# Weight forms and gated loads in SyncE's queue, the last gated stores in GpSimd's, at the turn between the two products of a gated layer

## The chip, the core and the metric

The kernel runs on one core of a Trainium2 chip. Its time is the device time of one launch in microseconds (us), as the median of several runs; the profile is of one further execution.

## What is computed

Attention with a positional decay, then two feed-forward layers on the 2304 tokens. The change lies in the last layer, whose reference is, word for word:

```
def _moe2_ref(x, w_in, w_out) -> np.ndarray:
    h = x @ w_in
    relu6 = np.clip(h + 3.0, 0.0, 6.0)
    g = h * relu6 / 6.0
    return (g @ w_out).astype(np.float32)
```

Here x is 2304 x 512, w_in 512 x 2048, w_out 2048 x 512. The weights of this layer come as 64-bit numbers and are decoded on the chip to 32-bit ones.

## The kernel before

**Two phases of one layer.** Both products of the layer are done in blocks of two by two with seven block products instead of eight (sums and differences of the blocks are formed first). Each 32-bit operand is split in a rounded high part and a low rest ("forms"); a block product is the sum of three TensorE products of these parts.

- In the first phase `unit(bi, k)` computes, for one of three groups of 768 tokens (bi) and one of eight slices of the hidden width (k), seven products of 6 matmuls each (line 1272, tiles `ws` and `xb`). Their results are collected by ACT and DVE (lines 1285 and 1291) and gated four times, `gate`: a relu on ACT (line 1298), a multiplication on DVE (line 1301), both in a tile `g` of a ring of six (`G_BUFS = 6`), and a store of 192 KB from that tile to the DRAM tensor `g_d` (line 1304). A tile of the ring is written again only when its store has landed. The last six units are those of the last two slices, k = 6 and 7, for bi = 0, 1 and 2; they have 24 gated stores.
- In the second phase `group(bi, t)` takes 128 columns of four gated blocks back from `g_d` (four loads `r11`, `r12`, `r21`, `r22`, line 1404; 512 KB each, in pieces of 512 bytes), forms sums (`n` and others, line 1412, on DVE), splits them (line 1424 on ACT, line 1428 on DVE or GpSimd) and multiplies them with the seven weight forms W0 to W6 (line 1447), 24 matmuls a product. There are nine groups. The results (`ob`) lie in tiles of the same ring `g` and are stored by line 1473.

**The weight forms** were made earlier and lie in DRAM: for W0, W1, W3 and W6 the unsplit blocks in `wt_d`, for W2, W4 and W5 (`SPLIT`) the split forms in `wp_d`. `weights(j)` loads each in three pieces. A piece of the first kind (256 or 384 KB, line 1353) goes to one of four staging places and is split by ACT and DVE (lines 1357 and 1360). A piece of the second kind (512 or 768 KB, line 1364) goes straight to its place. The places are the rooms of the first phase's operand forms `xb`, so a piece can come only when the last matmul that reads that room is done.

**Who issues, and in which order.** All instructions are collected with `plan.add(engine, us, function, ...)`, where `us` is a cost and `lag` the time until a result may be used; `emit` plays the plan through and writes each engine's instructions in the order of the planned starts. On the chip each engine's instructions then run in that order, each behind its waits. Before the change SyncE (SP) issues the gated stores, the gated loads and the output stores; GpSimd (POOL) issues all loads of weight forms. SyncE's transfers go through a hardware queue (q1 in the trace), GpSimd's through a software queue (q0); both run on the same 16 DMA engines.

Of the kernel before, what the change touches and what calls it, by code (L numbers as in the profile page):

```python
# [10 lines left out]
F32 = mybir.dt.float32  # L11
# [161 lines left out]
def dve(n):  # L173
    return 0.15 + 0.00104 * n
# [6 lines left out]
def act(n, extra=0.17):  # L181
    return extra + 0.00085 * n
# [6 lines left out]
def pe(n):  # L189
    return max(0.107, 0.000447 * n)  # L190
# [3 lines left out]
def kernel(ctx, tc, q, k, v, s, w_in, w_out, g_ln, w2_in, w2_out, out):  # L194
    nc = tc.nc
# [4 lines left out]
    P = 128  # L200
# [57 lines left out]
    def bank(key):  # L258
        return banks[plan.bank[key]]
# [124 lines left out]
    NK = KFF2 // 2  # L384
    T = {}
    wt_d = dram.tile([7, P, NK, 2 * P], F32, name="wt_d")
    wp_d = dram.tile([7, P, NK, 2, 2 * P], F32, name="wp_d")
    EARLY = (0,), (1, 2), (3, 4, 5)
    WT_PART = (0, 1, 2, 3, 4, 4, 6)
# [103 lines left out]
    plan = Plan()  # L493
# [619 lines left out]
    for b, share in enumerate(SHARES):  # L1113
        main = []
        if b == 0:
            first, second = pairs(False), pairs(True)
# [10 lines left out]
        while cost < share or in_sum:  # L1127
# [3 lines left out]
            c, f, _, in_sum = side.pop(pick)  # L1131
# [10 lines left out]
    g_d = dram.tile([NB, 2, 2, P, NK, W], F32, name="g_d")  # L1142
# [24 lines left out]
    def engine(name):  # L1167
        return {"DVE": nc.vector, "POOL": nc.gpsimd}[name]
# [15 lines left out]
    def x_form(bi, op):  # L1184
        return T[f"xb{bi}_{op}"]
# [74 lines left out]
    def unit(bi, k):  # L1260


        tag = f"{bi}_{k}"
        r = []

        def product(op, x, first):
            key = f"b{x}_{tag}"

            def mm():
                for kc in range(2):  # L1270
                    for i, (a, b) in enumerate(((0, 0), (1, 0), (0, 1))):
                        nc.tensor.matmul(bank(key)[:, :W], lhsT=T[f"ws{k}"][:, WS_OF[op], a, kc * P : (kc + 1) * P], rhs=x_form(bi, op)[:, b, kc, :],  # L1272
                                         start=(first and kc == 0 and i == 0), stop=(kc == 1 and i == 2), skip_group_check=not first)

            w = f"ws{k}"
            wk = {0: ["h0", "l0"], 1: ["h0", "l0"], 3: ["h768", "l768"], 5: ["s/h512", "s/l512"], 4: ["s/h512", "s/l512"]}.get(op, ["s/h0", "s/l0"])
            r.append(lambda: plan.add("PE", 6 * pe(W) + 0.01, mm, reads=[f"{w}/{y}" for y in wk] + [f"xb{bi}_{op}/{y}" for y in "hl"], writes=[key],
                                      bank=key if first else None))

        def keep(name, x):  # L1280
            key, to = f"b{x}_{tag}", f"{name}{tag}"

            def go():
                T[to] = pools["mid"].tile([P, W], F32, tag=name, name=to, bufs=2)
                nc.scalar.copy(T[to], bank(key)[:, :W])  # L1285

            r.append(lambda: plan.add("ACT", act(W), go, reads=[key, "second"], writes=[to], new=[(name, 2, to)]))

        def plus(name, x):
            key, to = f"b{x}_{tag}", f"{name}{tag}"  # L1290
            r.append(lambda: plan.add("DVE", dve(W), lambda: nc.vector.tensor_add(T[to], T[to], bank(key)[:, :W]), reads=[key, to], writes=[to]))

        def gate(o, h, src_key, src, eng="DVE"):
            g = f"g{tag}_{o}{h}"

            def relu():
                T[g] = pools["g"].tile([P, W], F32, tag="g", name=g, bufs=G_BUFS)
                nc.scalar.activation(out=T[g], in_=src(), func=AF.Relu, bias=3.0, scale=1.0)

            def times():  # L1300
                engine(eng).scalar_tensor_tensor(out=T[g], in0=T[g], scalar=6.0, in1=src(), op0=ALU.min, op1=ALU.mult)

            def store():
                nc.sync.dma_start(out=g_d[bi, h, o, :, k, :], in_=T[g])

            r.append(lambda: plan.add("ACT", act(W), relu, reads=[src_key], writes=[g], new=[("g", G_BUFS, g)]))
            r.append(lambda: plan.add(eng, dve(W) if eng == "DVE" else 1.1, times, reads=[src_key, g], writes=[g], port=src_key[0] == "c"))
            r.append(lambda: plan.add("SP", 0.5, store, reads=[g], writes=[f"gd{bi}_{h}{o}/{k}"], lag=4.5))

        def gate_kept(o, h, name):  # L1310
            gate(o, h, f"{name}{tag}", lambda: T[f"{name}{tag}"], "POOL" if (o, h) in ON_POOL else "DVE")

        product(0, "x", True)
        keep("c11", "x")
        product(1, "y", True)
        plus("c11", "y")
        product(2, "x", False)
        gate_kept(0, 0, "c11")
        keep("c12", "x")
        product(4, "z", True)  # L1320
        product(5, "x", False)
        keep("c22", "x")
        plus("c22", "z")
        product(6, "z", False)
        gate_kept(1, 1, "c22")
        product(3, "x", False)
        plus("c12", "z")
        gate(1, 0, f"bx_{tag}", lambda: bank(f"bx_{tag}")[:, :W])
        gate_kept(0, 1, "c12")
        return r  # L1330
# [5 lines left out]
    def weights(j):  # L1336


        i = SECOND[j][1]
        r = []  # L1340
        for q, (k0, k1) in enumerate(PIECES):
            key, number = f"W{i}_{q}", 3 * j + q
            pool, tag, _ = room(number)
            home = STAGE[number % len(STAGE)] if number < 3 * len(STAGE) - 4 else number % 2

            def load(key=key, k0=k0, k1=k1, home=home):
                if home in (0, 1):
                    if "stage" not in T:
                        T["stage"] = pools["xr"].tile([P, 2, 3, 2 * P], F32, tag="xr", name="stage", bufs=1)
                    T[f"{key}s"] = T["stage"][:, home, : k1 - k0]  # L1350
                else:
                    T[f"{key}s"] = pools["dec"].tile([P, k1 - k0, 2 * P], F32, tag=home, name=f"{key}s", bufs=1)
                nc.gpsimd.dma_start(out=T[f"{key}s"], in_=wt_d[i, :, k0:k1])

            def high(key=key, pool=pool, tag=tag, m=k1 - k0):
                T[key] = pools[pool].tile([P, 3, 2, 2 * P], F32R, tag=tag, name=key)
                nc.scalar.copy(T[key][:, :m, 0, :], T[f"{key}s"])

            def low(key=key, m=k1 - k0):
                nc.vector.tensor_sub(T[key][:, :m, 1, :], T[f"{key}s"], T[key][:, :m, 0, :].bitcast(F32))  # L1360

            def both(key=key, k0=k0, k1=k1, pool=pool, tag=tag):
                T[key] = pools[pool].tile([P, 3, 2, 2 * P], F32R, tag=tag, name=key)
                nc.gpsimd.dma_start(out=T[key][:, : k1 - k0].bitcast(F32), in_=wp_d[i, :, k0:k1])

            n = 2 * P * (k1 - k0)
            if i in SPLIT:
                r.append(lambda both=both, key=key, k0=k0, k1=k1, number=number: plan.add(
                    "POOL", 0.8, both, reads=[f"wt{k}/{WT_PART[i]}" for k in range(k0, k1)], writes=[f"{key}/h", f"{key}/l"], new=[(f"rm{number}", 1, key)], lag=8.0, port=False))
                continue  # L1370
            r += [
                lambda load=load, key=key, k0=k0, k1=k1, first=["stage"] * (number == 0), ring=[("xr", 1, "stage")] * (number == 0) + [(f"stage{home}" if home in (0, 1) else home, 1, f"{key}s")]: plan.add(
                    "POOL", 0.8, load, reads=[f"wt{k}/{WT_PART[i]}" for k in range(k0, k1)], writes=[f"{key}s", *first], new=ring, after=["stage"], lag=4.5, port=False),
                lambda high=high, key=key, n=n, number=number: plan.add("ACT", act(n), high, reads=[f"{key}s"], writes=[f"{key}/h"], new=[(f"rm{number}", 1, key)]),
                lambda low=low, key=key, n=n: plan.add("DVE", dve(n), low, reads=[f"{key}s", f"{key}/h"], writes=[f"{key}/l"], port=True),
            ]
        return r
# [6 lines left out]
    def group(bi, t):  # L1384
# [4 lines left out]
        mine = slots  # L1389
        slots = dict(r11=mine["n"], r12=mine["r21"], r21=mine["r11"], r22=mine["r12"], n=mine["r22"])  # L1390
        key = lambda x: f"{x}_{tag}"
# [6 lines left out]
        def raw_new(x):  # L1398
            return [(RAW_TAGS[mine[x]], 1, key(x))]

        def load(x, h, o):
            def go():
                raw_tile(x)
                nc.sync.dma_start(out=T[key(x)], in_=g_d[bi, h, o, :, :, t * P : (t + 1) * P])

            return lambda: plan.add("SP", 0.6, go, reads=[f"gd{bi}_{h}{o}/{k}" for k in range(NK)] + (["forms"] if mine[x] == 4 else []), writes=[key(x)], new=raw_new(x), lag=3.5)

        def total(to, a, b, op):
            def go():
# [82 lines left out]
    k_pairs = [(0, 1), *((k,) for k in range(2, NK - 2)), (NK - 2, NK - 1)]  # L1492
# [69 lines left out]
```

## Time and profile before

| | us |
|---|---|
| three runs, median (lowest to highest) | 828.41 (827.96 to 831.32) |
| the profiled execution, its time | 825.79 |
| its span, first to last instruction | 824.0 |
| TensorE busy in the span | 779.4 |
| VectorE, ScalarE, GpSimd busy | 597.0, 469.2, 245.6 |

So 1.79 us of the profiled execution lie around its span, and it was 2.62 us below the median. The times in a trace are counted from the span's start. In the trace, "PE" is TensorE, "PEld" its weight loads, "DVE" VectorE, "ACT" ScalarE; an engine with a "q" behind it is its sequencer, which issues DMAs and waits. The first phase ends and the second begins at about 620 to 637 us.

### The profile page before, as it was taken

The page shows a single profiled execution, that of the slowest core. Times are in us where ns is not written, and L with a number is a line of the kernel's source. Part 1 is how long each engine was busy: PE and PEld are TensorE (multiplying, and loading weights), DVE is VectorE, ACT ScalarE, POOL GpSimd, SP SyncE. Part 2 cuts the span into 40 slices and gives each one's busy share as a digit, 9 for nine tenths or more (in the row PEclk, how much of TensorE's full clock was granted, in tenths as well). Part 3 has the DMA queues.
Part 4 walks back from the last instruction along what each step waited for, and adds up shares of the span by engine and source line. Part 5 has one row for each costly group of instructions (what it writes and reads, how often), then busy time and mean ns, then how long its engine had stood idle before and what let it go on. Part 6 is the DMA issues. An engine that isn't in the chain of part 4 may idle for free.

```text
span 824.0 us, 15897 instructions
## 1 busy us (share of the span) xinstructions
PE 779.4 (95%) x5560; PEld 707.2 (86%) x5560; DVE 597.0 (72%) x1367; ACT 469.2 (57%) x1046; POOL 245.6 (30%) x327
## 2 busy tenths in 40 slices
PE   3789999999999999999999999999994999999998
PEld 2556577898887988888899999999994999999998
DVE  3687889768876789666787888888882876666662
ACT  2575778766765677655474666666672434444441
POOL 2464645434641545343630000000121002222222
PEclk9999999999999999999999999999996999999999
DMA  6753588698658866724333545666598644444440
GB/s 154 192 153 124 126 215 204 173 220 217 156 141 206 214 155 165 200 58 141 112 113 120 178 157 182 230 203 215 174 316 298 177 125 129 135 129 128 129 135 26
DMA packets 158751, 136.40 MB, mean 166 GB/s; under 512 B 67568, under 2 KB 138224, under 8 KB 158672
## 3 DMA queue, kind: packets, MB, share of 16 engines
q1 hardware_dynamic: 154112, 116.52, 50.8%
q0 software_dynamic: 2256, 10.49, 3.9%
q10 hardware_dynamic: 2304, 8.39, 3.2%
q8 instruction: 44, 0.72, 0.4%
q14 instruction: 35, 0.29, 0.1%
HBM read 74.74 MB, written 39.39 MB: 139 GB/s over the span
## 4 chain that ended last, share of the span: by engine, by line
PE 78%; DMA 10%; DVE 6%; ACT 2%; issue 2%; POOL 1%; SPq 1%; DVEq 0%; POOLq 0%; ACTq 0%
PE bank L1447 18%; PE bank L1272 17%; PE bank L1032 11%; PE bank L945 11%; PE bank L840 5%; PE bank L811 5%; PE bank L743 4%; PE bank L716 3%; DMA g_d<-g 2%; PE bank L1011 2%; DMA rawi<-in_moe_w_in_dram 1%; PE bank L606 1%; DMA r<-g_d 1%; DMA x_d<-x2s 1%; DMA whole<-rows_d 1%
## 5 line engine op out<-in xcount | busy, mean ns | idle before, releaser
L1272 PE MATMUL bank<-xb,ws 128*128 128x384 f32 x1008 | 178.4, 337 | 12.5 <-ACT c L1285 12.5
L1272 PEld LDWEIGHTS bank<-xb,ws 128*128 128x128 f32 x1008 | 176.2, 189 | 13.4 <-ACT c L1285 13.4
L1447 PE MATMUL bank<-W,fs 128*128 128x256 f32 x864 | 107.5, 283 | 2.4 <-DVE ob L1467 1.6
L1447 PEld LDWEIGHTS bank<-W,fs 128*128 128x128 f32 x864 | 105.1, 192 | 3.1 <-DVE ob L1467 1.8
L759 POOL TENSOR_SCALAR y<-y,rsum 128x128 f32<-128x128 f32 (+4 forms) x120 | 73.5, 630 | 101.6 <-DVE rsum L755 41.7
L664 DVE CUSTOM_DVE_ANT_0 y<-bank,mask 96x288 f32<-96x288 f32 (+4 forms) x168 | 74.0, 466 | 39.1 <-PE bank L743 22.4
L676 ACT ACTIVATE y<-y,nmax 128x384 f32<-128x384 f32 (+4 forms) x140 | 83.4, 597 | 31.0 <-DVE nmax L664 19.4
L1032 PE MATMUL bank<-zh,w_out_h 128*128 128x256 f32 x288 | 83.4, 290 | 0.2 <-ACT zh L1014 0.2
L1447 PE MATMUL bank<-W,fa 128*128 128x256 f32 x648 | 81.4, 283 | 0.5 <-ACT c L1456 0.5
L1032 PE MATMUL bank<-zl,w_out_h 128*128 128x256 f32 x288 | 80.9, 281 | 0.2 <-DVE zl L1018 0.2
L1032 PE MATMUL bank<-zh,w_out_l 128*128 128x256 f32 x288 | 80.9, 281 | 0.0
L1447 PEld LDWEIGHTS bank<-W,fa 128*128 128x128 f32 x648 | 79.7, 192 | 0.7 <-ACT c L1456 0.7
L945 PE MATMUL bank<-w_in_h,xh 128*128 128x512 f32 x144 | 61.3, 426 | 0.8 <-DVE xh L927 0.8
L743 PE MATMUL bank<-stack 128*96 128x288 f32 (+4 forms) x288 | 57.9, 318 | 2.5 <-DMA x_d<-x2s 1.1
L945 PE MATMUL bank<-w_in_h,xl 128*128 128x512 f32 x144 | 57.3, 398 | 0.6 <-POOL xl L931 0.6
L945 PE MATMUL bank<-w_in_l,xh 128*128 128x512 f32 x144 | 57.3, 398 | 0.0
L1032 PEld LDWEIGHTS bank<-zh,w_out_h 128*128 128x128 f32 x288 | 54.2, 188 | 2.4 <-ACT zh L1014 0.5
L1032 PEld LDWEIGHTS bank<-zh,w_out_l 128*128 128x128 f32 x288 | 54.3, 188 | 0.5
L1032 PEld LDWEIGHTS bank<-zl,w_out_h 128*128 128x128 f32 x288 | 54.3, 188 | 0.4 <-DVE zl L1018 0.4
L811 PE MATMUL bank<-ident,y 128*128 128x128 f32 (+2 forms) x420 | 50.8, 258 | 3.8 <-DVE pt4b L815 1.8
L1428 DVE TENSOR_TENSOR fs<-r,fs 128x1024 fp32r<-128x1024 f32 x27 | 38.9, 1446 | 19.9 <-ACT fs L1424 19.8
L1424 ACT CAST fs<-r 128x1024 fp32r<-128x1024 f32 x27 | 28.3, 1047 | 43.3 <-PE bank L1447 16.3
(256 smaller groups left out, 1553.8 us busy)
## 6 DMA issues: line engine op xcount, KB each, us to landing
g_d<-g SPq DMA_DIRECT2D x96, 192.0 KB, 2.3
r<-g_d SPq DMA_DIRECT2D x36, 512.0 KB, 5.7
rawo<-in_moe_w_out_dram SPq DMA_DIRECT2D x16, 512.0 KB, 3.5
rawi<-in_moe_w_in_dram SPq DMA_DIRECT2D x16, 512.0 KB
rawq<-in_q_dram SPq DMA_DIRECT2D x32, 144.0 KB, 4.0
rawk<-in_k_dram SPq DMA_DIRECT2D x32, 144.0 KB, 3.6
x_d<-x2s SPq DMA_DIRECT2D x36, 128.0 KB, 3.6
xr<-x_d SPq DMA_DIRECT2D x6, 768.0 KB, 4.7
```

What stands on the lines that cost most here:

```text
L664: nc.vector.tensor_tensor_reduce(out=ys[h, t][:n, c0:c1], in0=bank(key)[:n, : c1 - c0], in1=mask[:n, 480 + n - w + c0 : 480 + n - w + c1], ...
L676: nc.scalar.activation(out=y[:n], in_=y[:n], func=AF.Exp, bias=nmax[:n, h, t : t + 1], scale=-1.0, accum_out=sums[:n, h, t : t + 1])
L743: nc.tensor.matmul(bank(key)[:n, : c1 - c0], lhsT=ss[:, 2 - 2 * m, ST[t] : w], rhs=ss[:, 3 - 2 * m, c0:c1], start=(m == 0), stop=(m == 1))
L759: nc.gpsimd.tensor_scalar(ys[h, t][:n], ys[h, t][:n], rsum[:n, h, t : t + 1], 1.0, ALU.mult, ALU.mult)
L811: nc.tensor.transpose(bank(key)[: SZ[jj], c : c + SZ[t]], ys[h, t][: SZ[t], ST[jj] : ST[jj] + SZ[jj]], ident[: SZ[t], : SZ[t]])
L840: nc.tensor.matmul(bank(key)[j * D : (j + 1) * D, lo - c0 : c1 - c0], lhsT=vs[v_key(p, a)][:n, jj, j, :], rhs=pts[pt_key(2 * p + j, a)][:n ...
L945: nc.tensor.matmul(bank(key), lhsT=xs[i][m // 2][:, kk, :], rhs=(w_in_l if m == 1 else w_in_h)[:, kk, f * 512 : (f + 1) * 512], start=(kk ...
L1032: nc.tensor.matmul(bank(key)[:, : 2 * P], lhsT=w_out_at(w, kk)[:, m * P : (m + 1) * P], rhs=z[:, kk, :], start=(kk == 0 and i == 0), stop= ...
L1272: nc.tensor.matmul(bank(key)[:, :W], lhsT=T[f"ws{k}"][:, WS_OF[op], a, kc * P : (kc + 1) * P], rhs=x_form(bi, op)[:, b, kc, :], start=(fir ...
L1424: nc.scalar.copy(T[name][:, 0], T[key(src)])
L1428: lambda: plan.add(low, took(low, NK * P), lambda: engine(low).tensor_sub(T[name][:, 1], T[key(src)], T[name][:, 0].bitcast(F32)), reads=[ ...
L1447: nc.tensor.matmul(bank(b_key)[:, : 2 * P], lhsT=T[name][:, y, k, :], rhs=T[f"W{i}_{q}"][:, k - k0, w, :], start=first and k == 0 and y == ...
```

## The change

Loads of weight forms are issued by SyncE and not by GpSimd; the gated stores of the last two slices (k = 6 and 7) are issued by GpSimd and not by SyncE. The planned costs follow: a load on SyncE now takes the planner's queue for the time of its bytes, a gated load 1.6 and not 0.6 us.

```
@@ -1300,12 +1300,14 @@
+            ask, issue = ("POOL", nc.gpsimd) if k in k_pairs[-1] else ("SP", nc.sync)
+
             def store():
-                nc.sync.dma_start(out=g_d[bi, h, o, :, k, :], in_=T[g])
+                issue.dma_start(out=g_d[bi, h, o, :, k, :], in_=T[g])
...
-            r.append(lambda: plan.add("SP", 0.5, store, reads=[g], writes=[f"gd{bi}_{h}{o}/{k}"], lag=4.5))
+            r.append(lambda: plan.add(ask, 0.55, store, reads=[g], port=False, writes=[f"gd{bi}_{h}{o}/{k}"], lag=4.5))
@@ -1350,7 +1352,7 @@
-                nc.gpsimd.dma_start(out=T[f"{key}s"], in_=wt_d[i, :, k0:k1])
+                nc.sync.dma_start(out=T[f"{key}s"], in_=wt_d[i, :, k0:k1])
@@ -1361,16 +1363,16 @@
-                nc.gpsimd.dma_start(out=T[key][:, : k1 - k0].bitcast(F32), in_=wp_d[i, :, k0:k1])
+                nc.sync.dma_start(out=T[key][:, : k1 - k0].bitcast(F32), in_=wp_d[i, :, k0:k1])
...
-                    "POOL", 0.8, both, reads=[f"wt{k}/{WT_PART[i]}" for k in range(k0, k1)], writes=[f"{key}/h", f"{key}/l"], new=[(f"rm{number}", 1, key)], lag=8.0, port=False))
+                    "SP", 0.0032 * 2 * P * (k1 - k0), both, reads=[f"wt{k}/{WT_PART[i]}" for k in range(k0, k1)], writes=[f"{key}/h", f"{key}/l"], new=[(f"rm{number}", 1, key)], lag=2.5))
...
-                    "POOL", 0.8, load, reads=[f"wt{k}/{WT_PART[i]}" for k in range(k0, k1)], writes=[f"{key}s", *first], new=ring, after=["stage"], lag=4.5, port=False),
+                    "SP", 0.0016 * 2 * P * (k1 - k0), load, reads=[f"wt{k}/{WT_PART[i]}" for k in range(k0, k1)], writes=[f"{key}s", *first], new=ring, after=["stage"], lag=2.5),
@@ -1403,7 +1405,7 @@
-            return lambda: plan.add("SP", 0.6, go, reads=[f"gd{bi}_{h}{o}/{k}" for k in range(NK)] + (["forms"] if mine[x] == 4 else []), writes=[key(x)], new=raw_new(x), lag=3.5)
+            return lambda: plan.add("SP", 1.6, go, reads=[f"gd{bi}_{h}{o}/{k}" for k in range(NK)] + (["forms"] if mine[x] == 4 else []), writes=[key(x)], new=raw_new(x), lag=3.5)
```

What this does to the order of the queues, at three places. In the rows below a name ends in a running number of the tile (`r_0_0_6982` is a load of group bi = 0, t = 0); lines of the changed kernel stand two higher.

SyncE before, at the turn, from the first gated load on:

```order
L1404 DMA r_0_0_6982<-g_d 128x8x128
L1304 DMA g_d<-g_7_01_6990 128x384
L1304 DMA g_d<-g_6_00_6995 128x384
L1304 DMA g_d<-g_6_11_7004 128x384
L1304 DMA g_d<-g_6_10_7008 128x384
L1404 DMA r_0_0_7056<-g_d 128x8x128
L1304 DMA g_d<-g_6_01_7041 128x384
L1304 DMA g_d<-g_7_00_7045 128x384
L1404 DMA r_0_0_7072<-g_d 128x8x128
L1404 DMA r_0_0_7105<-g_d 128x8x128
L1304 DMA g_d<-g_7_11_7115 128x384
L1304 DMA g_d<-g_7_10_7117 128x384
```

and in the changed kernel, from the same load on:

```order
L1406 DMA r_0_0_6994<-g_d 128x8x128
L1355 DMA W_0s<-wt_d 128x768
L1406 DMA r_0_0_7056<-g_d 128x8x128
L1406 DMA r_0_0_7078<-g_d 128x8x128
L1355 DMA stage<-wt_d 128x768
L1366 DMA W_0_7105<-wp_d 128x1536
L1406 DMA r_0_0_7137<-g_d 128x8x128
L1355 DMA stage<-wt_d 128x512
L1366 DMA W_1_7165<-wp_d 128x1536
L1366 DMA W_2_7194<-wp_d 128x1024
```

The gated stores between the four gated loads are gone from SyncE; pieces of weight forms stand there, and one 768 KB piece stands ahead of the fourth gated load.

SyncE in the changed kernel, a little later, where the loads of the second group (`r_0_1`) follow (before the change they followed the last gated store):

```order
L1366 DMA W_0_7212<-wp_d 128x1536
L1366 DMA W_2_7239<-wp_d 128x1024
L1366 DMA W_0_7254<-wp_d 128x1536
L1366 DMA W_1_7283<-wp_d 128x1536
L1366 DMA W_1_7308<-wp_d 128x1536
L1366 DMA W_2_7332<-wp_d 128x1024
L1406 DMA r_0_1_7348<-g_d 128x8x128
L1406 DMA r_0_1_7367<-g_d 128x8x128
L1475 DMA out_dram<-ob_0_0_7372 128x256
```

All nine pieces from `wp_d` now stand in one queue with the second group's gated loads, and ahead of them.

GpSimd before, the last loads of weight forms:

```order
L1353 DMA W_0s<-wt_d 128x768
L1353 DMA stage<-wt_d 128x768 x2
L1364 DMA W_0_7093<-wp_d 128x1536
L1364 DMA W_1_7113<-wp_d 128x1536
L1353 DMA stage<-wt_d 128x512
L1364 DMA W_2_7165<-wp_d 128x1024
```

and in the changed kernel, the first of the 24 gated stores of the last units:

```order
L1306 DMA g_d<-g_6_00_6809 128x384
L1306 DMA g_d<-g_6_11_6853 128x384
L1306 DMA g_d<-g_6_10_6862 128x384
L1306 DMA g_d<-g_6_01_6879 128x384
L1306 DMA g_d<-g_7_00_6909 128x384
```

GpSimd issues nothing but these stores there. SyncE's two earliest pieces (in the middle of the first phase) stand between two gated stores of an earlier slice.

## Rows read from the trace of the kernel before

**Rows 1.** The page: busy time, and TensorE and the DMA engines in 40 slices.

```profile
PE 779.4 (95%) x5560; PEld 707.2 (86%) x5560; DVE 597.0 (72%) x1367; ACT 469.2 (57%) x1046; POOL 245.6 (30%) x327
...
PE   3789999999999999999999999999994999999998
...
DMA  6753588698658866724333545666598644444440
```

**Rows 2.** Busy time by stretch (the first line names the columns).

```profile
core 0: us, PE busy (x) PEld busy (x) DVE busy (x) ACT busy (x) POOL busy (x), PEclk, DMA share, GB/s
600.00:620.00 20.00, 20.00 (x120) 20.00 (x119) 14.46 (x25) 11.89 (x23) 5.40 (x10) 1.00 1.01 331
620.00:630.00 10.00, 0.61 (x6) 0.41 (x4) 0.00 (x0) 0.00 (x0) 0.02 (x1) 0.67 1.04 392
630.00:635.00 5.00, 2.44 (x8) 2.44 (x9) 2.65 (x5) 2.45 (x6) 0.00 (x0) 0.50 0.40 144
```

**Rows 3.** Waits, 610 to 680 us: who for whom, total us, times, longest.

```profile
ACT g L1298 <- DMA g_d<-g: 13.0, 1, 13.0
...
PE bank L1272 <- ACT c L1285: 12.0, 1, 12.0
```

**Rows 4.** SyncE's timeline around the turn: start, us, line, transfer, count.

```profile
605.53 4.93 SPq L1404 DMA_DIRECT2D r<-g_d  x2
610.55 14.49 SPq L1304 DMA_DIRECT2D g_d<-g  x1
...
643.78 1.54 SPq L1404 DMA_DIRECT2D r<-g_d  x2
```

**Rows 5.** DMA queues, 618 to 626 us: packets, MB, share of 16 engines.

```profile
q0 software_dynamic: 624, 2.89, 91.5%
q1 hardware_dynamic: 620, 0.32, 13.3%
```

**Rows 6.** DMA queues, 604 to 640 us.

```profile
DMA packets 6473, 10.98 MB, mean 305 GB/s; under 512 B 445, under 2 KB 5221, under 8 KB 6470
...
q0 software_dynamic: 1425, 6.76, 55.2%
q1 hardware_dynamic: 5045, 4.19, 34.9%
```

**Rows 7.** DMA issues, 570 to 584 us, little traffic: count, KB, us to landing.

```profile
q1 hardware_dynamic: 1209, 1.66, 33.3%
...
g_d<-g SPq DMA_DIRECT2D x9, 192.0 KB, 1.9
W_0s<-wt_d POOLq DMA_DIRECT2D x1, 384.0 KB, 3.5
```

**Rows 8.** Instructions on tile W, 600 to 641 us: ns least/median/most.

```profile
L1364 POOL DMA_DIRECT2D W<-wp_d x9: 540/540/546, 607.2 to 637.1; - x9
```

**Rows 9.** GpSimd's timeline, 560 to 690 us.

```profile
689.04 2.40 POOL L1428 TENSOR_TENSOR fa<-r,fa 128x1024 fp32r<-128x1024 f32 x1 [4.79 <-ACT fa L1424]
```

**Rows 10.** TensorE's timeline, 632 to 665 us.

```profile
632.57 4.21 PE L1272 MATMUL bank<-xb,ws 128*128 128x384 f32 x12 [11.95 <-ACT c L1285]
636.57 3.71 PE L1447 MATMUL bank<-W,fa 128*128 128x256 f32 x28
...
650.99 2.34 PE L1447 MATMUL bank<-W,fa 128*128 128x256 f32 x18
```

**Rows 11.** DMA queues, 646 to 654 us.

```profile
q1 hardware_dynamic: 4155, 2.20, 97.2%
```

**Rows 12.** Instructions on tile r, 640 to 690 us.

```profile
L1424 ACT CAST fa<-r x7: 1039/1040/1054, 648.8 to 687.9; 128x1024 fp32r<-128x1024 f32 x7
```

**Rows 13.** Instructions on tile g, 560 to 600 us.

```profile
L1298 ACT ACTIVATE g<-c x18: 508/526/538, 560.5 to 599.3; 128x384 f32<-128x384 f32 x18
L1301 DVE SCALAR_TENSOR_TENSOR g<-g,c x17: 547/551/559, 561.5 to 599.6; 128x384 f32<-128x384 f32 x17
```

**Rows 14.** Timeline of all engines, 462 to 486 us.

```profile
478.65 0.95 DVE L1214 TENSOR_TENSOR xb<-xr,xb 128x768 fp32r<-128x768 f32 x1
...
480.19 1.34 POOL L1353 DMA_DIRECT2D stage<-wt_d  x2 [47.97 <-DMA g_d<-g]
```

## The prediction

> **What bounds the kernel now.** I read the page first: TensorE is busy for 95% of the span, and after the start only one of the 40 slices is weak, the 32nd, where the DMA engines' digit is among the highest [rows 1]. So TensorE sets the time nearly everywhere, and the question is what stops it there. The busy times by stretch show it: 20.00 of 20 us at 600 to 620, then 0.61 of 10 us at 620 to 630, while the DMA share is 1.04 and all other engines are idle; after that the granted clock is 0.50, the 1.2 GHz level [rows 2]. The waits name the chain: TensorE waited 12.0 us once for a result copy of ACT, and ACT 13.0 us once for a gated store that should have freed a tile of the ring `g` [rows 3]. SyncE's timeline says why that store was late: SyncE issued two gated loads at 605.53, and then one gated store blocked its issue for 14.49 us, from 610.55 to 625.04 [rows 4]. The queues between 618 and 626 us say why it blocked. Packets of the two queues alternate (624 against 620), but a packet of weights is 2.89 MB / 624 = 4.63 KB and one of SyncE's queue 0.52 KB, so the weights got 2.89 MB and the gated loads, with the stores behind them, 0.32 MB [rows 5]. The stores stood behind small pieces in a queue that moved a tenth of the bytes. Transfers as a whole aren't the stop: what had to be stored was little, and it was in the wrong line.
>
> **What goes.** The hole is 11.95 us, and the 12 matmuls behind it take 4.21 us [rows 10]; at the pace of 120 in 20 us [rows 2], 0.1667 us each, they take 2.0. Hole and slow clock together are 11.95 + 2.2 = about 14.2 us, and the phase end moves from 636.57 to about 622.4. This holds in full if none of the last 24 stores is late enough to stop ACT again.
>
> **The stores on GpSimd.** Each costs GpSimd about 0.54 us of issue, as its weight loads do (540/540/546 ns) [rows 8]; they leave GpSimd in exchange, and GpSimd is only 30% busy [rows 1]. Gates come every 42 x 0.1667 / 4 = 1.75 us, so the issue keeps up: cost nothing, covered by TensorE's own 1.75 us. The landing is what counts. On a quiet stretch a store on SyncE landed in 1.9 us and a weight load on GpSimd in 3.5 us [rows 7]. Under load I use the alternation: a store's packet is 1.66 MB / 1209 = 1.37 KB [rows 7], a weight piece's 4.63 KB [rows 5], so against weights alone the stores get 1.37 / 6.00 = 0.23 of about 400 GB/s (2.89 + 0.32 MB in 8 us), 91 GB/s; they want 0.197 MB / 1.75 us = 112 GB/s. In the 18 us from 604 to 622 that leaves them 21 x 18 = 0.38 MB behind, two stores or 3.4 us. Landing 3.5 + 3.4, plus relu and multiplication 0.53 + 0.55 [rows 13], is 8.0 us; six tiles cover 6 x 1.75 = 10.5 us. So no hole, cost 0. The lower end is 0 and the upper 4 us (a store that lands some 3 us later than this would cost a first hole). Against SyncE's 512 byte loads the stores fare better, and those are in the same stretch; so I take 0.
>
> **The weights on SyncE.** Two early pieces now stand between gated stores. Their room comes free at 478.65 + 0.95 = 479.60, where the `xr` tile was read last, and GpSimd issued them at 480.19, when nothing held it but that [rows 14]; a store behind them can wait about 1 us, and the ring covers it: 0, at most 1 us. At the turn SyncE may wait for rooms, but no store of slices 6 and 7 stands behind it there. The gated load `r22`, last of its four, has a 768 KB piece before it: from 604 the queue holds two gated loads, a 384 KB piece, this piece and `r22`, 2.74 MB; at 331 GB/s [rows 2] less the stores' 112 they take 12.5 us, to 616.5, ahead of the new phase end 622.4. Cost 0.
>
> **What is late next.** The same bytes must pass the same 16 engines in a stretch that is 14 us shorter. From 604 to 640 the two queues held 55.2% + 34.9% = 90.1% of 36 us, 32.4 us of work, 10.98 MB [rows 6]. At the share of 1.04 that the engines showed when full [rows 2] this ends at 604 + 32.4 / 1.04 = 635.2. The second group's loads (`r_0_1`) were issued at 643.78 [rows 4], after all that; now they would go at 629.6, but behind all pieces in the same queue. The first of them, 0.524 MB, takes 1.85 us at the pace of 2.20 MB in 8 us [rows 11], so 637.0; it is done about 1.4 us later (1.9 us landing of a store [rows 7] less about 0.5 for its bytes at 400 GB/s), and ACT's rounding takes 1.04 us [rows 12]: 639.5. TensorE wants it where its group at 650.99 begins [rows 10], now 636.8. It is 2.7 us late; that is the one thing I give back. Ends: 0, if the engines run fuller than this, and 5 us, if the rooms free the last pieces later and the second load of the pair counts as well.
>
> **The sum**, against the profiled execution's own 825.79 us (span 824.0 and 1.79 around it): 825.79 - 14.2 + 2.7 = 814.3. It was 2.62 us below the median of the three runs, so in terms of the median 816.9 us.
>
> **Rivals.**
> (1) *The wait only moves; the time stays.* All bytes stay and run on the same engines, at a share over 1 already; if `r22` or a weight form lands only when all pieces have (635), the first product that needs it stops TensorE for about 635.2 - 622.4 = 12.8 us, and the time is near 827. For it speaks the full share, against it the order, which puts only one piece of 768 KB ahead of `r22` (above). A rule speaks for this rival: the Trainium skill, page "DMA: Bandwidth & Descriptors", section "Issuing engines are not separate DMA queues", says that transfers started by different engines end on the same 16 DMA engines and that issuing from several saves only the sequencers' time to start them. By that rule alone the time stays near 828.4. Rows 5 contradict its "only": which queue a transfer stands in decided a share of 9 to 1 of the bytes.
> (2) *Slower: GpSimd's issue stretches and paces the end of the phase.* Twenty-four stores in a row on an engine that computes too; if issue plus wait took t for each, TensorE would be held to t and not 1.75 us a gate. All is lost at 24 x (t - 1.75) = 11.5 (14.2 less 2.7), t = 2.23 us. At 2.5 us the time is 816.9 + 24 x 0.75 = 834.9. The near row is 0.54 us for the same kind of issue [rows 8]; the far one is a GpSimd addition that took 2.40 us [rows 9]. It would have to come to the far end, and GpSimd's part in gating is small there (0 to 5.40 us of work in the stretches [rows 2]). The Trainium skill, same page, section "SWDGE vs HWDGE vs iDMA", says that GpSimd writes its descriptor rings in SBUF, which VectorE in its two-port mode locks it out of. Rows 8, six nanoseconds between least and most, do not show that here.
> (3) *Half given back.* Stores land slower than reckoned (over 10.5 less 1.1 us, against SyncE's transfers), one or two holes of 2 to 3 us come, and `r_0_1` is 5 us late: 814.2 + 5 + 4 = 823.2.
> (4) *All of it stays*: `r_0_1` is in time, 828.41 - 14.2 = 814.2.
>
> **How the numbers follow.** Forecast with what lies between (3) and (4), that is 814 to 820: 0.70; (3), 820 to 824.3: 0.16; (1), no change: 0.09; (2): 0.05. About 0.5% or 4.1 us is what a measurement here can tell from no change, so faster means below 824.3: 0.70 + 0.16 = 0.86; same 0.09; slower 0.05. The range begins at 825.79 - 14.2 = 811.6, which holds if the runs of the changed kernel lie at the level of the profiled execution, with nothing given back, and ends at 823.2, the sum of all upper bounds; outside are rivals 1 and 2 and little of 3. The likeliest time is 816.9.
>
> **What would show it.** In the changed kernel's profile TensorE is without a hole from 600 to 622, ACT no longer waits for a gated store, and the granted clock stays at 1.00 through the turn. GpSimd's store issues take 0.54 to 0.55 us and their stores land in at most 9 us in the loaded stretch. SyncE still has long issues there, but only ahead of loads. A wait of 2 to 4 us stands near 636 to 640 on TensorE, ended by the forms of `r_0_1` and through them by its load. Wrong would be: a wait of ACT for a store again (the ring), a wait for `r22` or for a weight form of 5 us or more right behind the phase end (rival 1), GpSimd's issues over 1.75 us (rival 2), or a second group whose loads land before 636 (then nothing is given back).

## The result and the profile after

The changed kernel takes 816.14 us (median of 5 runs, 815.51 to 818.95) beside 828.79 us for the kernel before: a ratio of 0.9854, 95% interval 0.9829 to 0.9878. The forecast was 816.9 us. The profiled execution took 818.13 us. The change saved 828.79 - 816.14 = 12.65 us by the medians, but the two profiled executions differ by only 825.79 - 818.13 = 7.66 us. The next rows show why, and give a finer measure.

TensorE's matmuls of the first phase (line 1272) and of the second (line 1447 before, 1449 after, with the `fa` forms that end the program), in the whole trace of the kernel before. Columns are line, engine, operation and tiles, count, ns of least/median/most, first and last start in us, form.

```profile
L1272 PE MATMUL bank<-xb,ws x1008: 333/334/689, 426.7 to 636.3; 128*128 128x384 f32 x168
...
L1447 PE MATMUL bank<-W,fa x648: 278/283/415, 619.0 to 820.7; 128*128 128x256 f32 x162
```

The same of the changed kernel:

```profile
L1272 PE MATMUL bank<-xb,ws x1008: 333/334/444, 430.4 to 630.5; 128*128 128x384 f32 x168
...
L1449 PE MATMUL bank<-W,fa x648: 278/283/384, 623.9 to 812.8; 128*128 128x256 f32 x162
```

From the first matmul of the layer to the last it took 820.7 - 426.7 = 394.0 us before and 812.8 - 430.4 = 382.4 us after: 11.6 us less. The rest is how late the layer began, 426.7 against 430.4, ahead of anything that the change touches; it varies from profile to profile (between 426.2 and 432.5 in all kernels below). This **layer time** is used below beside the medians. In a second profile of the changed kernel it was 811.0 - 428.4 = 382.6 us.

Busy time by stretch in the changed kernel (columns as in [rows 2]):

```profile
600.00:620.00 20.00, 18.48 (x106) 17.96 (x105) 15.50 (x27) 13.58 (x27) 6.43 (x12) 1.00 0.94 308
620.00:630.00 10.00, 8.51 (x55) 8.23 (x53) 5.32 (x11) 3.88 (x9) 2.14 (x4) 1.00 1.04 410
630.00:635.00 5.00, 3.81 (x29) 3.60 (x29) 4.63 (x6) 3.02 (x5) 1.62 (x3) 1.00 1.04 395
```

Where TensorE had worked 0.61 of 10 us [rows 2] it now works 8.51, and the granted clock stays at 1.00. From 620 to 630 us the DMA engines are as full as before, 1.04. But TensorE isn't without holes. Its timeline in the changed kernel (start, us, line, operation, count, idle time before and what ended it):

```profile
619.60 4.47 PE L1272 MATMUL bank<-xb,ws 128*128 128x384 f32 x24 [1.52 <-ACT c L1285]
623.91 0.87 PE L1449 MATMUL bank<-W,fa 128*128 128x256 f32 x6
626.27 1.31 PE L1272 MATMUL bank<-xb,ws 128*128 128x384 f32 x6 [1.49 <-ACT c L1285]
...
632.99 3.14 PE L1449 MATMUL bank<-W,fa 128*128 128x256 f32 x24 [1.19 <-ACT fa L1426]
...
645.15 2.34 PE L1449 MATMUL bank<-W,fa 128*128 128x256 f32 x18
```

Three holes of 1.52, 1.49 and 1.19 us stand at the turn, 4.2 us together. ACT's timeline in the changed kernel shows what is behind the first two:

```profile
618.34 0.83 ACT L1359 CAST W<-stage 128x768 fp32r<-128x768 f32 x1 [2.36 <-DMA stage<-wt_d]
619.08 0.85 ACT L1285 COPY c<-bank 128x384 f32<-128x384 f32 x2
...
624.40 0.62 ACT L1359 CAST W<-stage 128x512 fp32r<-128x512 f32 x1 [2.83 <-DMA stage<-wt_d]
624.92 0.93 ACT L1298 ACTIVATE g<-c 128x384 f32<-128x384 f32 x2
625.76 0.46 ACT L1285 COPY c<-bank 128x384 f32<-128x384 f32 x1
```

ACT stood 2.36 and 2.83 us before the split of a staged weight piece that hadn't landed, and the copies behind it, which free TensorE's banks, came late: matmuls went on at 619.60 and 626.27. Twenty of GpSimd's 24 gated stores in the changed kernel, those from 596 us on:

```profile
L1306 POOL DMA_DIRECT2D g_d<-g x20: 539/539/542, 596.6 to 633.3; - x20
...
DMA to landing us min/median/max: 3.3/5.8/7.4
```

Issue takes 539 to 542 ns (the first of all 24, ahead of these, took 753) and the slowest landing 7.4 us. In this profile ACT waits for no store any more. In the second profile (`after_again`) it does once:

```profile
606.95 0.52 ACT L1298 ACTIVATE g<-c 128x384 f32<-128x384 f32 x1 [1.54 <-DMA g_d<-g]
```

No hole of TensorE stands behind that wait.

### The profile page after: what moved, and what is told of

It reads as the page before. It is cut to its first block, busy times and chain, and to the rows that moved or that the text cites. A ratio compares the mean times of both kernels' runs of the same rounds, so it can differ in the third digit from the quotient of the medians.

```text
span 816.3 us, 15900 instructions
## 1 busy us (share of the span) xinstructions
PE 780.7 (96%) x5560; PEld 707.1 (87%) x5560; DVE 597.2 (73%) x1367; ACT 468.9 (57%) x1046; POOL 245.3 (30%) x330
## 4 chain that ended last, share of the span: by engine, by line
PE 85%; DMA 5%; DVE 4%; POOL 2%; ACT 2%; issue 1%; SPq 1%; POOLq 0%; DVEq 0%; ACTq 0%
PE bank L1449 22%; PE bank L1272 19%; PE bank L1032 12%; PE bank L945 10%; PE bank L840 6%; PE bank L811 5%; PE bank L743 5%; PE bank L716 3%; PE bank L1011 2%; PE bank L606 1%; POOL y L777 1%; DMA stage<-wt_d 1%; DMA rawi<-in_moe_w_in_dram 1%; DMA whole<-rows_d 1%; DMA rows_d<-neg 1%
## 5 line engine op out<-in xcount | busy, mean ns | idle before, releaser
L1272 PEld LDWEIGHTS bank<-xb,ws 128*128 128x128 f32 x1008 | 174.4, 188 | 5.3 <-ACT c L1285 5.2
L1306 POOL DMA_DIRECT2D g_d<-g x24 | 13.1, 549 | 185.7 <-DVE g L1301 185.7
```

## The experiments

The change has three parts: the weights' queue, the stores' queue, and the planned costs, which set the order in a queue. Twelve runs took it apart: ten kernels, one of them twice, and the changed kernel once more. Each was set beside the kernel before on the same chip; ratios are to that.

**1. Stores alone** (`stores_only`), against the kernel before:

```
-                nc.sync.dma_start(out=g_d[bi, h, o, :, k, :], in_=T[g])
+            ask, issue = ("POOL", nc.gpsimd) if k in k_pairs[-1] else ("SP", nc.sync)
...
+                issue.dma_start(out=g_d[bi, h, o, :, k, :], in_=T[g])
```

> The changed kernel with all loads of weight forms back on GpSimd, and the planned costs of all loads as before: of the change only the last 24 gated stores on GpSimd are left, among the weight pieces. Before 828.8, changed 816.1. Theory (the 12 us hole came from stores behind 512-byte gated loads in SyncE's queue): the stores now wait for at most one or two 768 KB pieces ahead of them, 2.2 us each at 2.89 MB in 8 us, and land in 6 to 9 us, so the hole is gone or down to 3 us: 814 to 820. Rival (the gain comes from the weights, whose large packets no longer take the engines from SyncE's queue): the time stays at 825 to 829.

Measured: 828.02 us, ratio 1.0013 (0.9988 to 1.0038), layer time 824.2 - 430.8 = 393.4 us: no gain, the time of the rival. TensorE's timeline and the waits of this kernel:

```profile
627.79 3.51 PE L1449 MATMUL bank<-W,fa 128*128 128x256 f32 x28
643.40 1.65 PE L1449 MATMUL bank<-W,fs 128*128 128x256 f32 x6 [12.11 <-ACT fs L1426]
...
DVE n L1414 <- DMA r<-g_d: 15.5, 2, 12.5
```

and its DMA queues from 624 to 628 us (packets, MB, share of 16 engines):

```profile
q0 software_dynamic: 346, 1.48, 91.8%
q1 hardware_dynamic: 302, 0.15, 12.7%
```

The first phase now ends without the hole, since the stores are with the weights. The hole has moved behind it, with the same size: the sum `n` waits for a gated load. SyncE's queue, which now holds nothing but 512-byte gated loads there, still got only 0.15 of 1.63 MB. That the cure is to take the stores out of SyncE's queue is refuted. They were what showed the starved queue first; the gated loads were next.

**2. Weights alone, with the new planned costs** (`weights_only`), against the kernel before (here and in 3 for both kinds of pieces):

```
-                nc.gpsimd.dma_start(out=T[f"{key}s"], in_=wt_d[i, :, k0:k1])
+                nc.sync.dma_start(out=T[f"{key}s"], in_=wt_d[i, :, k0:k1])
-                nc.gpsimd.dma_start(out=T[key][:, : k1 - k0].bitcast(F32), in_=wp_d[i, :, k0:k1])
+                nc.sync.dma_start(out=T[key][:, : k1 - k0].bitcast(F32), in_=wp_d[i, :, k0:k1])
```

> The changed kernel with the last 24 gated stores back on SyncE: of the change only the weight loads on SyncE and the planned costs are left. Theory (stores must not stand behind gated loads in one queue): the stores still stand behind gated loads and now behind weight pieces too; a hole on TensorE of 4 to 12 us stays, ended by a store that frees a tile of g: 820 to 828. Rival (it was the two queues' competition): with one queue the gated loads pass quickly and the stores with them; no hole, 813 to 817.

Measured: 815.73 us, ratio 0.9849 (0.9818 to 0.9880), layer time 813.0 - 432.5 = 380.5 us. The rival of this run is right. Its queues from 612 to 628 us:

```profile
q1 hardware_dynamic: 4918, 5.41, 103.2%
```

and TensorE's timeline:

```profile
621.64 2.38 PE L1272 MATMUL bank<-xb,ws 128*128 128x384 f32 x12 [0.21 <-ACT c L1285]
624.64 1.33 PE L1272 MATMUL bank<-xb,ws 128*128 128x384 f32 x6 [0.63 <-ACT c L1285]
```

Weights, gated loads and stores, 5.41 MB, went through one queue in the order in which it was filled; the stores still stand behind gated loads there, and ACT waits for none of them.

Repeated beside the changed kernel on one chip (`after_again`, `weights_only_again`):

> The changed kernel once more, beside the next run on the same chip: 0.985 of the time before, as measured, within 0.004.

> The run weights_only once more, beside the changed kernel on the same chip. Theory after the first runs (the move of the weights is the whole gain, the move of the stores nothing): the same time as the changed kernel within 0.3%. Rival (the stores on GpSimd help by what the two holes of the changed kernel hide): slower than the changed kernel by 2 us or more.

Measured: 0.9875 (0.9846 to 0.9904) for the changed kernel, 0.9865 (0.9838 to 0.9891) without the move of the stores; layer times 382.6 and 813.2 - 431.8 = 381.4 us. The move of the stores is worth nothing here; by the layer times it costs 1 to 2 us, little more than the scatter.

**3. Weights alone, with the old planned costs** (`weights_old_costs`), and the changed kernel with the old planned costs (`old_costs`), whose diff against the changed kernel has this line among others:

```
-            return lambda: plan.add("SP", 1.6, go, reads=[f"gd{bi}_{h}{o}/{k}" for k in range(NK)] + (["forms"] if mine[x] == 4 else []), writes=[key(x)], new=raw_new(x), lag=3.5)
+            return lambda: plan.add("SP", 0.6, go, reads=[f"gd{bi}_{h}{o}/{k}" for k in range(NK)] + (["forms"] if mine[x] == 4 else []), writes=[key(x)], new=raw_new(x), lag=3.5)
```

> The kernel before with one thing changed: all loads of weight forms are issued by SyncE. Stores stay on SyncE and all planned costs are as before, so only the queue of the weights differs and the order on SyncE that follows. Theory (the hole came from two queues that alternate by packets, 4.63 KB of weights against 0.52 KB of gated loads): one queue is enough, no hole over 2 us on TensorE at the turn, 814 to 818, like the run with the new costs (815.7). Rival (the new planned costs, which give the order of need, are the gain): a gated store or load comes behind too many pieces, a hole of 5 us or more, 820 to 828.

> The changed kernel with the planned costs of all loads as before; both queues are as in the change (weights on SyncE, last 24 stores on GpSimd). Weights on SyncE with old costs and stores on SyncE took 818.3, with a hole of 2.4 us and ACT waiting 3.1 us for a store. Theory (stores in a queue of their own cannot be late behind an unfavourable order on SyncE, so the move of the stores is worth something only where the order is bad): 815.5 to 817.5, no wait of ACT for a store. Rival (the order of the loads itself costs, through staged pieces and gated loads, whoever issues the stores): 818 to 822.

Measured: 818.33 us, ratio 0.9906 (0.9885 to 0.9927), layer time 812.9 - 426.2 = 386.7 us; and 820.87 us, 0.9914 (0.9887 to 0.9941), 817.1 - 430.5 = 386.6 us. The first lies just above its theory's range and below its rival's, the second with its rival. So the order that comes of the costs is a part of its own, and the move of the stores doesn't replace it. With the old order each has one late transfer at the turn. The waits of `weights_old_costs`:

```profile
ACT g L1298 <- DMA g_d<-g: 3.1, 1, 3.1
```

and of `old_costs`, where the store is out of the way and a staged piece is late instead:

```profile
ACT W L1359 <- DMA stage<-wt_d: 6.9, 2, 5.4
```

Layer times of the combinations, in us (two values are two profiles, which puts the scatter at about 1 us):

| | stores on SyncE | last stores on GpSimd |
|---|---|---|
| weights on GpSimd, old costs | 394.0 | 393.4 |
| weights on SyncE, old costs | 386.7 | 386.6 |
| weights on SyncE, new costs | 380.5, 381.4 | 382.4, 382.6 |

With the weights in SyncE's queue the layer takes some 7 us less, with the new order in it some 4 to 6 us less again, and with the stores' queue nothing less. The new costs with the weights left on GpSimd weren't run, so what the order is worth is shown only for weights on SyncE.

**4. Is it the packets?** `small_packets` is the kernel before with each straight piece in two loads of 512-byte elements:

```
-                nc.gpsimd.dma_start(out=T[key][:, : k1 - k0].bitcast(F32), in_=wp_d[i, :, k0:k1])
+                for a in range(2):
+                    nc.gpsimd.dma_start(out=T[key][:, : k1 - k0].bitcast(F32).rearrange("p m x (a f) -> p a (m x) f", f=P)[:, a], in_=wp_d[i, :, k0:k1].rearrange("p m x (a f) -> p a (m x) f", f=P)[:, a])
```

> The kernel before, with the nine straight weight pieces cut in elements of 512 bytes (two loads for each piece, still on GpSimd). The same bytes, queues and order. Theory (the queues take turns packet by packet, so the size of a packet sets the share): SyncE's queue gets about half and not a tenth of the bytes, SyncE's issue that blocked for 14.49 us falls below 6 us, and ACT's wait of 13.0 us for a store falls below 4 us; the weights become late in exchange, and the time may be anything from 816 to 832. Rival (GpSimd's queue goes first whatever its packets are): the block stays at 12 us or more and the wait of ACT too.

Measured: 835.98 us in one run. The queues between 618 and 626 us:

```profile
q0 software_dynamic: 602, 2.08, 88.0%
q1 hardware_dynamic: 647, 0.33, 18.3%
```

The edit didn't make small packets: 2.08 MB / 602 = 3.46 KB each, down from 4.63. By its signs the rival came out: one SyncE issue was blocked for 13.4 us (from 615.85), and ACT waited longer for a store than before:

```profile
ACT g L1298 <- DMA g_d<-g: 18.3, 1, 18.3
PE bank L1272 <- ACT c L1285: 17.2, 1, 17.2
```

But with packets of 3.46 KB against 0.51 the first theory expects a starved SyncE queue too, so the time can't decide between the two as it was meant to. TensorE's hole grew to 17.2 us, while the weights moved more slowly (2.08 against 2.89 MB in 8 us). The counts do bear on it. They show the turns again, 602 against 647, and SyncE's queue got 0.33 MB whether the other moved 2.89 or 2.08. Its share rose from 10% [rows 5] to 0.33 / 2.41 = 14%, near to what the packets' sizes give, 0.51 / (0.51 + 3.46) = 13%.

`act_queue` is the kernel before with the straight pieces on ACT's queue, which is a hardware queue like SyncE's:

```
-                nc.gpsimd.dma_start(out=T[key][:, : k1 - k0].bitcast(F32), in_=wp_d[i, :, k0:k1])
+                nc.scalar.dma_start(out=T[key][:, : k1 - k0].bitcast(F32), in_=wp_d[i, :, k0:k1])
```

> The kernel before, with the nine straight weight pieces issued by ACT, through a second hardware queue, and not by GpSimd; staged pieces stay on GpSimd. Theory (any two queues take turns packet by packet): packets of the two queues come in like numbers while both are full, SyncE's queue again gets 0.1 to 0.2 of the bytes, and a gated store or load is late by 8 us or more: 822 to 836. Rival (only GpSimd's queue holds SyncE's back): SyncE's queue keeps half of the bytes or more, the block of 14.5 us on SyncE falls below 5 us, and the time is 814 to 820 plus what ACT loses by issuing.

Measured: 826.50 us in one run. Queues from 632 to 640 us (q10 is ACT's):

```profile
q10 hardware_dynamic: 531, 2.57, 77.6%
q1 hardware_dynamic: 573, 0.77, 26.1%
```

Two hardware queues moved like numbers of packets as well, 531 against 573. In this stretch SyncE's queue held stores of larger packets, 0.77 MB / 573 = 1.34 KB, and got 23% of the bytes, close to what the packets' sizes give, 1.34 / (1.34 + 4.84) = 22%. That much of the theory stands. The time, 826.50, is in the theory's range, but it is no measure of it. ACT's own issues stood waiting (until 623.65 and 636.96) with its copies and roundings behind them, which made two holes of 4.1 and 5.2 us on TensorE. The longest block of a store's issue on SyncE was 6.2 us (from 615.67), between what the two theories expected.

**5. The two holes of the changed kernel.** `stage_lag` lets the planner reckon more time for a staged piece:

```
-                    "SP", 0.0016 * 2 * P * (k1 - k0), load, reads=[f"wt{k}/{WT_PART[i]}" for k in range(k0, k1)], writes=[f"{key}s", *first], new=ring, after=["stage"], lag=2.5),
+                    "SP", 0.0016 * 2 * P * (k1 - k0), load, reads=[f"wt{k}/{WT_PART[i]}" for k in range(k0, k1)], writes=[f"{key}s", *first], new=ring, after=["stage"], lag=6.0),
```

> The changed kernel, but the planner reckons 6.0 us and not 2.5 us until a staged weight piece is there. No engine or queue changes, only the order: on ACT the splits of the last three staged pieces move behind one or two copies and relus of the gates. Theory (the holes of 1.69 and 1.60 us that the changed kernel has at 619.6 and 626.3 come from ACT waiting 2.4 and 2.8 us for a staged piece, with the copy that frees TensorE's bank queued behind it): both holes shrink to under 0.6 us each and the time falls by 2 to 3.3 us, to 813 to 814. Rival (the pieces are late in any case, and the product that needs them stops as long): the wait moves to the product of the second phase, 815.5 to 817.

Measured: 818.31 us, ratio 0.9886 (0.9853 to 0.9919), layer time 811.5 - 428.5 = 383.0 us, so nothing gained. (The holes of 1.69 and 1.60 us in the expectation are the 1.52 and 1.49 us above.) ACT's timeline, TensorE's, and the busy times by stretch in this kernel:

```profile
628.02 0.62 ACT L1359 CAST W<-stage 128x512 fp32r<-128x512 f32 x1 [1.91 <-DMA stage<-wt_d]
...
629.23 1.03 ACT L1426 CAST fa<-r 128x1024 fp32r<-128x1024 f32 x1
...
630.32 4.53 PE L1449 MATMUL bank<-W,fa 128*128 128x256 f32 x24 [2.75 <-ACT fa L1426]
...
630.00:635.00 5.00, 4.68 (x27) 4.68 (x28) 4.97 (x5) 2.83 (x4) 0.54 (x1) 0.66 1.03 423
```

The copies come in time and both holes are gone, but ACT still waits 1.91 us for the last staged piece, now with a rounding of the second phase behind it, and one hole of 2.75 us takes their place. Behind this one the granted clock is 0.66 from 630 to 635 us: it was at 0.50, the 1.2 GHz level, for part of that stretch. The 24 matmuls there take 4.53 us, in the changed kernel (632.99) 3.14. So 2.75 + 1.39 = 4.1 us are lost, as much as by the three shorter holes, behind which the clock stayed at 1.00. The rival is right that the wait moves; its range, 815.5 to 817, was too low.

`stage_pool` issues the staged pieces by GpSimd again (line 1355, with the old cost):

> The changed kernel with the staged weight pieces (256 and 384 KB) issued by GpSimd as before, while the pieces that go straight to their place stay on SyncE. Theory (staged pieces are late because they stand behind 512-byte gated loads in SyncE's queue): on GpSimd they land in 4 to 6 us, ACT does not wait for them, and the holes at 619.6 and 626.3 are gone: 812.5 to 814.5. Rival (the engines are full and every piece is as late in either queue, or the stores behind the pieces become late): 815.5 to 819, with a wait of ACT for a gated store.

Measured: 816.70 us, 0.9867 (0.9839 to 0.9895), layer time 811.5 - 430.1 = 381.4 us, about 1 us less than the changed kernel. The theory's time, 812.5 to 814.5, wasn't reached. The two holes are down to one of 0.5 us, but one of 1.75 us comes up at 643.78, ended by a form of a later product:

```profile
618.08 4.47 PE L1272 MATMUL bank<-xb,ws 128*128 128x384 f32 x24 [0.47 <-ACT c L1285]
...
643.78 2.41 PE L1449 MATMUL bank<-W,fa 128*128 128x256 f32 x18 [1.75 <-ACT fa L1426]
```

`weights_lag`, which joins `weights_only` with the larger lag, was the try for the best version:

> All weights and all gated stores on SyncE with the new planned costs (the run that took 815.7), and the planner reckons 6.0 us and not 2.5 us until a staged piece is there, so that ACT's splits stand behind the copies. Theory (what is left at the turn is ACT waiting for staged pieces ahead of copies, 0.8 and 0.4 us in that run): 1 us less, 814 to 815.5. Rival (the wait moves to the first forms of the second phase, as it did in the run stage_lag): 815.5 to 818.

Measured: 816.69 us, 0.9879 (0.9856 to 0.9901), layer time 810.4 - 429.7 = 380.7 us. The hole before the rounding `fa` is still there, 1.19 us; the time is in the rival's range. No version is faster than the changed kernel by more than its runs scatter.

**6. The ring.** `ring5_after`: `G_BUFS = 5` in the changed kernel.

> The changed kernel with five and not six tiles in the ring g. The prediction reckoned landing plus gate at 8.0 us, the trace of the changed kernel shows landings of 3.3 to 7.4 us, with 1.1 us for the gate up to 8.5; five tiles cover 5 x 1.75 = 8.75 us. If that reckoning holds, the time rises by 0 to 1.5 us, to 816 to 817.7. If the stores' landing is nearer to the limit than reckoned (gates come in pairs, so a tile is wanted sooner than the mean says): ACT waits for gated stores, several holes of 1 to 3 us, 819 to 824.

Measured: 819.40 us, 0.9909 (0.9890 to 0.9928), layer time 817.9 - 432.0 = 385.9 us, some 3.4 us more than with six tiles: the second of the two readings in the expectation. ACT's timeline in it:

```profile
618.56 0.53 ACT L1298 ACTIVATE g<-c 128x384 f32<-128x384 f32 x1 [1.42 <-DMA g_d<-g]
...
620.44 0.53 ACT L1298 ACTIVATE g<-c 128x384 f32<-128x384 f32 x1 [0.48 <-DMA g_d<-g]
621.27 0.53 ACT L1298 ACTIVATE g<-c 128x384 f32<-128x384 f32 x1 [0.31 <-DMA g_d<-g]
```

With five tiles ACT waits for stores three times, 2.2 us together; with six not at all in one profile and once in the other (1.54 us, with no hole). Part of the 3.4 us is the clock: behind a hole of 2.37 us it is 0.66 from 630 to 635 us, and 12 matmuls take 3.92 us that take 2.25 in the changed kernel. The mean rate of one gate in 1.75 us is too kind: most of GpSimd's stores from 603 us on come in twos and fours.

## Why the prediction was right, and where it wasn't

**The term that carries it holds.** Hole and slow clock were put at 14.2 us. The hole of 11.95 us is gone, and the granted clock is 1.00 through the turn. The net of 14.2 - 2.7 = 11.5 us stands beside 11.6 us of layer time. But the 11.6 is made up otherwise than reckoned, so the closeness is in part luck.

**The cause was named only by half.** The prediction read the alternation of packets in [rows 5] and drew from it that what was to be stored "was in the wrong line". The runs show that the line didn't matter: the stores alone gave nothing, the weights, with their new planned costs, everything. The alternation was right; what it starves is a queue, with all that is in it, and the cure is to take the large packets out of the other queue.

**Rival 1 was real, one part of the change away.** A wait that moves to the gated load, near 827 us, is what `stores_only` did (12.5 us, 828.02). In the change itself the weights' move removed it, as the prediction argued from the order. The Trainium skill, page "DMA: Bandwidth & Descriptors", section "Issuing engines are not separate DMA queues", says that issuing from several engines saves only the time to start transfers. `weights_old_costs` moved the same bytes over the same engines, in one queue (and so in another order) and not in two, and took 7.3 us off the layer, so that "only" isn't borne out here. The Trainium skill, same page, section "SWDGE vs HWDGE vs iDMA", says that each DMA engine goes round between the queues that feed it. The counts agree in four stretches where both queues were full: 624 against 620 [rows 5], 346 against 302, 602 against 647, 531 against 573. They don't in one, 759 against 297 (the last section).

**The stores on GpSimd at cost 0.** Issue 0.54 us and landings of at most 7.4 us plus 1.1 for the gate, 8.5 us, against a reckoned 8.0: right. The cover of 10.5 us was too kind (`ring5_after`), and six tiles just held: the wait of ACT for a store, which the prediction names as a sign of being wrong, came once in the second profile, without a hole on TensorE.

**The weights on SyncE at cost 0: the step that failed.** The text looked for stores behind the weights on SyncE and found none at the turn. It didn't ask who waits for the staged pieces, which now stand behind gated loads: ACT, with the copies behind it. Two holes came of it, 1.52 + 1.49 us, and `stage_lag` shows that a later place of the split only moves the wait. The weights' move alone doesn't make these holes. With the stores left on SyncE (`weights_only`) ACT waits for the staged pieces too,

```profile
ACT W L1357 <- DMA stage<-wt_d: 3.8, 2, 2.6
```

against 5.2 us in the changed kernel, but TensorE stops for only 0.21 and 0.63 us, and in the repeat for nothing there. So the 3 us come only with the last stores in GpSimd's queue beside it, and the prediction put both moves at nothing; whether through the bytes that the stores take or through the order on ACT stays open. A third hole, 1.19 us, is ended by a rounding of the first group (`fa`, at 631.91 on ACT, behind the last gates); nothing of the kind was reckoned.

**The 2.7 us given back at the second group didn't come.** TensorE went into the group of 18 at 645.15 without a stop. Its loads were issued at 637.75, which in the prediction's time (the layer began 3.7 us later in this execution) is 634.1 and not 629.6. SyncE issued its last piece of weights by 632.17 and then waited 5.5 us for DVE's `fs` of the first group:

```profile
SPq L1406 <- DVE fs L1430: 11.8, 5, 5.5
```

Before the change the same loads waited for the same `fs` (4.3 us). So they left 4.5 us later than reckoned because the first group came later, by about what the holes had cost, 4.2. ACT's wait for the first of them ended at 643.25. In the prediction's time that is 639.5 instead of 638.4, so the landing was well reckoned, although the issue wasn't. What failed is when it is wanted: 641.4 in that time and not 636.8, as the holes ahead had already cost 4.2 us. The loss that was priced here was paid earlier, for another transfer. (One division in that sum is wrong: 0.524 MB at 2.20 MB in 8 us take 1.91 us, not 1.85, which changes nothing that shows.)

**The remainder.** 14.2 less the three holes of 4.2 leaves 10.0, and the layer gained 11.6. In the trace of before TensorE waits once more, for a result copy (`ob`):

```profile
675.11 3.14 PE L1447 MATMUL bank<-W,fs 128*128 128x256 f32 x24 [1.62 <-DVE ob L1467]
```

The changed kernel doesn't have that wait, and 10.0 + 1.6 = 11.6. The prediction has no term for it. It goes with the planned costs: all six kernels with the old costs have such a wait (0.2 to 1.6 us), none of those with the new cost of a gated load. What in the order removes it wasn't followed up.

**Rival 2** needed issues of over 2.2 us; 539 to 542 ns were measured in twenty stores and 753 ns in the longest of all 24, and no lock-out of GpSimd shows.

## What to carry to other kernels

Where two queues are full, ask for each how large its packets are. In four stretches here the two queues moved like numbers of packets, so the one with the small packets got 9 to 23% of the bytes, as the packets' sizes give, and everything behind them waited. Moving the one transfer whose wait the profile names may only show the next one in the same queue, as in `stores_only`; here it helped to put the bulk transfer into that queue instead, at the place where it is needed. Then go through every engine that waits for what was moved, in its own order: in the changed kernel it was not the late piece of weights that stopped TensorE, but the copies that stood behind its split on ACT.

## What was not expected

- GpSimd's queue joined elements: loads written as 512-byte elements left in packets of 3.46 KB, and the queue moved 2.08 instead of 2.89 MB in 8 us.
- The start of the layer lay between 426.2 and 432.5 us in the profiles of these kernels, though nothing ahead of it was edited. Two single profiles can thus differ by 6 us for reasons that have nothing to do with a change; for a late change, a stretch that begins behind the scatter measures better.
- In `stores_only` the turns hold from 624 to 628 us, but from 628 to 636 the software queue moved 759 packets and SyncE's 297, though a gated load was under way until 641. What held SyncE's queue back further there stays open.
